# An adaLN, spectral-filter and bilinear-GLU block, forward and backward, on one core: TensorE's order in the tail written down as one chain, with filler dealt per step

## The chip, the cores and the metric

The kernel runs on one core of a Trainium2 chip. The metric is the time of one execution in microseconds of device time; where several executions were timed, the median is given. The engines are named as the profile names them: PE (TensorE, matmul), PEld (its weight loads), DVE (VectorE), ACT (ScalarE), POOL (GpSimd) and SP (SyncE, which here only issues transfers). "SPq" and "POOLq" are the queues of transfers that SP and POOL issue.

## The reference

The reference is the forward pass of one block and the gradients of all its inputs (jax.vjp), on x of 2048 rows by 576 columns in bfloat16, F = 4608:

```
mod = (silu(c) @ w_mod) split into sa, ca, ga, sb, cb, gb
h = layernorm(x) * (1 + ca) + sa
x = x + ga * irfft2(rfft2(h) * (w_r + i w_i))
h = layernorm(x) * (1 + cb) + sb
x = x + gb * (((h @ w_gate) * (h @ w_up)) @ w_down)
_out, _vjp = jax.vjp(_f, A_x, A_w_r, A_w_i, B_w_gate, B_w_up, B_w_down, c, w_mod)
```

The outputs are the result (out_0) and the gradients of x (out_1), w_r and w_i (out_2, out_3), w_gate and w_up (out_4, out_5), w_down (out_6), c (out_7) and w_mod (out_8).

## The kernel before, in words

The 2048 rows are 16 tiles of 128 (t = 0 to 15), the 4608 columns of the inner dimension 36 blocks of 128. All matmuls are bfloat16 with a 128 x 128 stationary tile. The Fourier transforms are matmuls with tables (T_RD, T_G, T_BD, T_BDA, T_GB, T_IR).

The first 284 us hold the norms, the forward transform and its filter, and the gradient that comes through w_down (u4p). From 284 to 1246.7 a loop runs over the 36 blocks: gate and up products (gup), the three weight-gradient products of earlier blocks (u57p, line 599: of hh, gg and gu, 32 matmuls each, 16 row tiles by two halves of 288 columns), and the gradient of the normed input (u8p, line 681), which VectorE adds into an f32 accumulator, line 686. Each block's hh goes out to DRAM (hhT_d), since the forward down projection needs all blocks.

What the change touches lies behind the last gate and up product:

- **The last accumulation**: the u8p of the last two blocks, together, for 16 tiles and 2 halves (128 matmuls, 32 additions on VectorE).
- **The backward norm**, a pipeline over the 16 tiles with four steps: `t1_norm` (loads of n2c, goc and yc on SP; norm gradient on VectorE and ScalarE), `t1_turn` (transposes trp, line 897; column sums csA, csB, csC, lines 800 and 807), `t1_cols` (products with T_RD, zp, line 917) and `t1_rows` (products with T_G, vp, lines 924 and 925). At t = 1 `t1_norm` also loads T_RD and multiplies its five slices by ga, line 885, on VectorE.
- **The held products**: the 192 u57p matmuls of the last two blocks are issued as filler beside the backward norm. Their outputs are cast by ScalarE and stored, those of gg and gu over a transposing transfer (woT, lines 610 to 612).
- **The spectral filter**, a pipeline over 19 chunks of four groups: `t2_turn` (transposes trv), `t2_filter` (xp; on VectorE products fm with the filter wn, line 198, which is loaded again from DRAM), `t2_back` (transposes), `t2_inv` (apt), `t2_grad` (for every fourth chunk the gradient of the filter, lines 963 to 972). The other 14 chunks' gradients are computed later (`more_grads`), beside the down projection.
- **The inverse transform**, a pipeline over 16 tiles with `t3_rows` (upa, upb), `t3_cols` (yp) and `t3_norm` (norm gradient, out_1, column sums csD, csE).
- **The down projection**: for each tile 72 matmuls (u3p, line 1129), two halves by 36 blocks. w_down lies in wdA (blocks 0 to 14) and wdB (15 to 35); hh comes back in pieces hl, four to two tiles, of nine blocks each. Then out_0, products for the gradient of gb, and `section`, which writes the six parts of the gradient of w_mod, five of them beside the projection (`late`) and the last at the very end.

The order on each engine comes from a planner of the tile framework: it takes instructions by priority (`tc.high_priority` with HEAD_START = 350 and SPREAD = 40 per step in the backward norm) and fills the gaps of one stage with ready work of another. `tc.issue_after(x)` keeps an instruction behind x. In the backward norm the list `fill` holds the last matmul of each group of held products, and `behind(fill[t - 1:t])` ties the zp of tile t to one of them, so that 16 held matmuls go between neighbours. SP's queue is in order: an issue that waits holds all behind it. The loads of hl and w_down are issued by SP, behind `after` (the yc load of tile 5):

```
wd_load(dst, k, f0, n, behind_=None):
    with tc.issue_after(behind_ or after):
        nc.sync.dma_start(dst[:, k:k + n, :], B_w_down[...])
```

Of the kernel before, what the change touches and what calls it, by code (L numbers as in the profile page):

```python
# [19 lines left out]
NT = 16  # L20
# [64 lines left out]
def build(ctx, tc, A_x, A_w_r, A_w_i, B_w_gate, B_w_up, B_w_down, c_in, w_mod, grad_out,  # L85
# [46 lines left out]


    cnt = [0]

# [51 lines left out]

    def pipeline(n, steps):

        for k in range(n + len(steps) - 1):  # L190
            for s_ in reversed(range(len(steps))):
                if 0 <= k - s_ < n:
                    steps[s_](k - s_)

    def spectral_products(m1, Z, wn, f0, w):
# [347 lines left out]
    with ExitStack() as ms:  # L543
# [14 lines left out]
        with ExitStack() as bs:  # L558
# [27 lines left out]
            nso = [0]  # L586
            fill = []

            def u57_items(sf, rhs_n, done):
                so = so4[:, nso[0] % NSO, :]  # L590
                nso[0] += 1
                items = []
                for h in range(2):
                    pw = []

                    def item(h, t, pw=pw):
                        if t == 0:
                            pw.append(u57ps.tile([128, 512], FP32, name="u57p", tag="x"))
                        mm = nc.tensor.matmul(pw[0][:, 0:288], lhsT=sf[:, t, :], rhs=rhs_n[:, t, h * 288:(h + 1) * 288], start=(t == 0), stop=(t == NT - 1))  # L599
                        if t == NT - 1:  # L600
                            fill.append(mm.ins)
# [124 lines left out]
            fill.clear()  # L726
# [9 lines left out]
    with ExitStack() as ts:  # L736
# [12 lines left out]
        zero = tl0.tile([128, 512], BF, name="zero")  # L749
        o2p = pool("o2p", 2)  # L750
        oAp = pool("oAp", 1)
        oBp = pool("oBp", 1)
# [38 lines left out]
        def wide(m):  # L791
# [64 lines left out]
        with ExitStack() as r1:  # L856
# [11 lines left out]
            def t1_norm(t):  # L868
                for k, src in (("n2c", n2_d), ("goc", go_v), ("yc", y_d)):
                    ld[k, t] = c1.tile([128, D], BF, name=k, bufs=5)  # L870
                    with behind(ld["order"]):
                        ins = nc.sync.dma_start(ld[k, t][:], src[:, t, :])
                if t == 5:
                    ld["after"] = ins.ins
                ld["final"] = ld["y", t] = ins.ins
                if t in (1, 2):
                    ld["order"] = [ins.ins]
                    with behind(ld["order"]):
                        for k, tag in ((("RD", "tA"),), (("G1", "tB"), ("BD2", None), ("BDA", None)))[t - 1]:
                            T[k] = load_table(tl0, k, tag)  # L880
                    ld["order"] = [tab_ins[k]]
                    if t == 1:
                        for m in range(5):
                            row = T["RD"][:, m].rearrange("p c f -> p (c f)")
                            nc.vector.tensor_scalar(out=row, in0=row, scalar1=ga_col[:, m:m + 1], scalar2=None, op0=MUL)
                n2 = ld["n2c", t][:]
# [24 lines left out]
            def t1_cols(t):  # L911
                zt = zts[t] = c1.tile([128, 2, FP], BF, name="zt")
                for cc in range(2):
                    zp = ps_fp.tile([128, 512], FP32, name="zp", tag="fp")
                    for m in range(5):
                        with behind(fill[t - 1:t] if t else []):
                            nc.tensor.matmul(zp[:, :FP], lhsT=gyTs[t][:, m, :], rhs=T["RD"][:, m, cc, :], start=(m == 0), stop=(m == 4))  # L917
                    nc.scalar.copy(zt[:, cc, :], zp[:, :FP])
# [10 lines left out]
            for k in range(NT + len(steps) - 1):  # L929
                with tc.high_priority(HEAD_START + SPREAD * k):  # L930
                    for s_ in reversed(range(len(steps))):
                        if 0 <= k - s_ < NT:
                            steps[s_](k - s_)
            after = ld["after"]
            dcb = diag_rows(tl, csA, csB, 288, "dcb")
# [10 lines left out]
        ra = pool("ra", 1, "right", stack=rA)  # L946
        wn = ra.tile([128, 2, NT, FP], BF, name="wn2")
        for c in range(2):
            with tc.issue_after(ld["final"]):
                nc.sync.dma_start(wn[:, c].rearrange("k a f -> k (a f)"), wn_d[:, c * NT * FP:(c + 1) * NT * FP])  # L950
        fg = pool("fg", 2, "right", stack=rA)
# [22 lines left out]
        with ExitStack() as r2:  # L974
# [95 lines left out]

        pipeline(NT, [t3_rows, t3_cols, t3_norm])
        dca = diag_rows(tl, csD, csE, 288, "dca")
# [8 lines left out]
        def more_grads(t):  # L1081
            for ci in rest[2 * (t - 2):2 * (t - 1)] if t >= 2 else []:
                with tc.issue_after(ld3["last"]):
                    filter_grad(ci)
            if t == 8:
                for which in range(2):
# [7 lines left out]

        late = {9: (MSB, of_sums(dsb)), 10: (MCB, of_rows(dcb)), 11: (MGA, of_rows(dga)), 12: (MSA, of_sums(dsa)), 13: (MCA, of_rows(dca))}


        csF = ps_cs.tile([128, 512], FP32, name="csF", tag="csB")
        wdA = oAp.tile([128, 15, D], BF, name="wdA")
        wdB = oBp.tile([128, NFB - 15, D], BF, name="wdB")  # L1100

        def wd_load(dst, k, f0, n, behind_=None):
            with tc.issue_after(behind_ or after):
                nc.sync.dma_start(dst[:, k:k + n, :], B_w_down[f0 * 128:(f0 + n) * 128, :].rearrange("(j f) d -> f j d", f=128))

        for k in range(0, 15, 5):
            wd_load(wdA, k, k, 5, ld["y", 7 + 2 * (k // 5)])
        prs = {}
        for tp_ in range(NT // 2):
            hls = []  # L1110
            for b0 in range(0, NFB, 9):
                nq = 4 * tp_ + b0 // 9
                hl = hlp.tile([128, 9, 256], BF, name="hl2") if nq >= 12 and (nq - 12) % 13 < 7 else o2p.tile([128, 9, 256], BF, name="hl", bufs=6)
                with tc.issue_after(after):
                    nc.sync.dma_start(hl[:], hhT_d[tp_, :, b0:b0 + 9, :])
                hls.append(hl)
                if tp_ == 0 and b0 in (9, 18):
                    wd_load(wdB, 10 * (b0 // 9 - 1), 15 + 10 * (b0 // 9 - 1), 9 + b0 // 9)
            x1t = o2p.tile([128, 2, D], BF, name="x1t3", bufs=1)
# [3 lines left out]
            for ti in range(2):  # L1123
                t = 2 * tp_ + ti
                ob = o2p.tile([128, D], BF, name="ob3")
                for h in range(2):
# [15 lines left out]
                more_grads(t)  # L1142
                if 8 <= t < 13:
                    for k in range(3 * (t - 8) if t < 12 else 12, min(16, 3 * (t - 7)) if t < 12 else 16):
# [84 lines left out]
```

## Time and profile before

| | |
|---|---|
| median of 3 runs | 1581.78 us (1580.73 to 1594.68) |
| the profiled execution | 1590.85 us |
| its span | 1589.1 us |
| PE busy | 1526.9 us (96%) |
| DVE busy | 1035.6 us (65%) |
| ACT busy | 551.5 us (35%) |
| POOL busy | 172.3 us (11%) |
| mean DMA rate over the span | 176 GB/s |
| mean granted PE clock | 0.993 |

The stages of the span begin at these times: last accumulation with the first norm steps 1246.7, the rest of the backward norm 1281.8, filter 1350.9, inverse transform 1413.9, down projection alone 1455.4, end section 1575.8.

In a row of the timeline the columns are start (us), duration (us), engine, line, operation, output and inputs, shape and count; in square brackets stands the idle time of the engine ahead of it and what ended it. Rows of groups have the summed busy time and the mean in ns, then the idle time ahead of the group's instructions. A busy PE is modelled: small gaps between matmuls do not show as idle. Windows give each engine's busy time, then the granted clock of PE as a share of full speed, the DMA engines' busy share and the rate.

### The profile page before, as it was taken

How to read it: one execution, taken by the hardware profiler on the slowest of the kernel's cores; microseconds unless marked ns; L12 is line 12 of the kernel's file. 1: busy time of each engine (PE TensorE's matmuls, PEld its weight loads, DVE VectorE, ACT ScalarE, POOL GpSimd, SP SyncE). 2: the span in 40 equal slices, each digit the busy share in tenths (PEclk: the TensorE clock that was granted, in tenths of full speed). 3: DMA queues.
4: the chain of work that ended last, by engine and by line, in shares of the span. 5: the costliest groups of instructions: out<-in, count | busy, mean ns of one | idle time of the engine just before them, and what ended most of it. 6: DMA issues, size and time to landing. Idle time of an engine off the chain costs nothing.

```text
span 1589.1 us, 30036 instructions
## 1 busy us (share of the span) xinstructions
PE 1526.9 (96%) x11299; PEld 1027.1 (65%) x11306; DVE 1035.6 (65%) x2632; ACT 551.5 (35%) x1136; POOL 172.3 (11%) x284
## 2 busy tenths in 40 slices
PE   6999889999999999999999999999999899899997
PEld 4666533566666676666667666666766566577775
DVE  6866653666666666666666666666666584678655
ACT  6667632322222222222222222222222255476022
POOL 0001212101010010101001010100100011100232
PEclk9999999999999999999999999999999999999998
DMA  9869998778778685785867777675856777646684
GB/s 319 270 196 245 238 242 227 159 150 148 143 140 164 125 168 116 162 155 113 166 136 150 146 151 135 145 160 115 169 122 131 204 200 211 234 151 224 244 239 143
DMA packets 491635, 280.19 MB, mean 176 GB/s; under 512 B 408897, under 2 KB 463810, under 8 KB 490466
## 3 DMA queue, kind: packets, MB, share of 16 engines
q1 hardware_dynamic: 466450, 187.75, 55.0%
q0 software_dynamic: 25040, 90.53, 19.0%
q8 instruction: 88, 1.44, 0.4%
q14 instruction: 57, 0.47, 0.1%
HBM read 108.33 MB, written 82.31 MB: 120 GB/s over the span
## 4 chain that ended last, share of the span: by engine, by line
PE 79%; DMA 9%; DVE 5%; issue 5%; ACT 1%; SPq 1%; POOL 0%; DVEq 0%; ACTq 0%; POOLq 0%
PE u57p L599 26%; PE u8p L681 18%; PE gup L652 16%; PE u4p L408 7%; PE u3p L1129 4%; PE gup L647 2%; DMA wdT<-wdn 2%; DMA Xn<-xn_d 2%; DMA wdB<-in_B_w_down_dram 1%; DMA xc<-in_A_x_dram 1%; DMA n2c<-n_d 1%; PE zp L346 1%; PE zp L917 1%; PE u4p L403 1%; DMA hh_sf<-hhT 1%
## 5 line engine op out<-in xcount | busy, mean ns | idle before, releaser
L686 DVE TENSOR_TENSOR acc<-acc,u8p 128x288 f32<-128x288 f32 x1088 | 489.3, 453 | 319.5 <-PE u8p L681 319.1
L681 PE MATMUL u8p<-wT,ggT 128*128 128x288 bf16 x1152 | 328.7, 287 | 4.4 <-DVE acc L686 4.4
L681 PE MATMUL u8p<-wT,guT 128*128 128x288 bf16 x1152 | 328.4, 287 | 0.0
L652 PE MATMUL gup<-h2T,wgu 128*128 128x512 bf16 x1152 | 294.9, 379 | 0.0
L602 ACT CAST so<-u57p 128x288 bf16<-128x288 f32 x216 | 86.0, 398 | 520.3 <-PE u57p L599 512.0
L599 PE MATMUL u57p<-h2p,gg_sf 128*128 128x288 bf16 x1152 | 189.2, 287 | 0.0
L599 PE MATMUL u57p<-gon,hh_sf 128*128 128x288 bf16 x1152 | 187.9, 286 | 0.3 <-DMA hh_sf<-hhT 0.3
L599 PE MATMUL u57p<-h2p,gu_sf 128*128 128x288 bf16 x1152 | 186.7, 286 | 0.0
L652 PEld LDWEIGHTS <-wgu 128*128 128x128 bf16 x1152 | 109.5, 98 | 98.8 <-issue 17.1
L408 PE MATMUL u4p<-goT,wdT 128*128 128x512 bf16 x656 | 152.7, 382 | 5.8 <-DVE ghh_st L143 5.3
L681 PEld LDWEIGHTS <-ggT 128*128 128x128 bf16 x1152 | 112.9, 98 | 67.4 <-issue 14.0
L681 PEld LDWEIGHTS <-guT 128*128 128x128 bf16 x1152 | 113.0, 98 | 58.4 <-issue 4.8
L1129 PEld LDWEIGHTS <-hl 128*128 128x128 bf16 x1152 | 112.0, 98 | 39.7 <-issue 10.4
L599 PEld LDWEIGHTS <-hh_sf 128*128 128x128 bf16 x1152 | 112.5, 98 | 28.9 <-DMA hh_sf<-hhT 0.6
L599 PEld LDWEIGHTS <-gg_sf 128*128 128x128 bf16 x1152 | 112.6, 98 | 28.5
L599 PEld LDWEIGHTS <-gu_sf 128*128 128x128 bf16 x1152 | 112.5, 98 | 28.5
L654 ACT CAST gT<-gup 128x512 bf16<-128x512 f32 x144 | 84.4, 586 | 130.7 <-PE gup L652 130.7
L408 PEld LDWEIGHTS <-wdT 128*128 128x128 bf16 x656 | 61.5, 98 | 79.1 <-issue 14.7
L654 ACT CAST uT<-gup 128x512 bf16<-128x512 f32 x144 | 84.3, 585 | 73.5 <-PE gup L652 73.5
L1129 PE MATMUL u3p<-wdB,hl 128*128 128x288 bf16 x672 | 92.7, 288 | 7.4 <-DMA wdB<-in_B_w_down_dram 7.4
L665 POOL DMA_DIRECT2D hhT_d<-hhT x36 | 33.2, 921 | 481.8 <-DVE hhT L656 452.8
L141 ACT CAST ghh_st<-u4p 128x512 bf16<-128x512 f32 x88 | 50.9, 585 | 65.3 <-PE u4p L408 64.3
(357 smaller groups left out, 1677.3 us busy)
## 6 DMA issues: line engine op xcount, KB each, us to landing
ghhT_d<-ghh_st POOLq DMA_DIRECT2D x36, 512.0 KB, 4.5
ghh<-ghhT_d POOLq DMA_DIRECT2D x36, 512.0 KB, 7.2
hhT_d<-hhT POOLq DMA_DIRECT2D x36, 512.0 KB, 6.5
hl<-hhT_d SPq DMA_DIRECT2D x32, 576.0 KB, 8.1
out_dram<-woT SPq DMA_DIRECT2D x72, 128.0 KB, 2.0
wdn<-in_B_w_down_dram SPq DMA_DIRECT2D x18, 288.0 KB, 3.6
out_dram<-so SPq DMA_DIRECT2D x36, 144.0 KB, 2.7
wgu<-in_B_w_gate_dram SPq DMA_DIRECT2D x18, 256.0 KB, 3.2
```

Source lines behind the costliest of these rows:

```text
L141: nc.scalar.copy(dst, src)
L346: mm = nc.tensor.matmul(zp[:, :FP], lhsT=hTs[t][:, m, :], rhs=T["RD"][:, m, cc, :], start=(m == 0), stop=(m == 4))
L408: nc.tensor.matmul(pt[:], lhsT=wdTs[k][:, j, m, :], rhs=goT[:, 4 * sb4:4 * sb4 + 4, m, :], start=(m == 0 and n == 5), stop=(m == n - 1))
L599: mm = nc.tensor.matmul(pw[0][:, 0:288], lhsT=sf[:, t, :], rhs=rhs_n[:, t, h * 288:(h + 1) * 288], start=(t == 0), stop=(t == NT - 1))
L602: nc.scalar.copy(so[:, h * 288:(h + 1) * 288], pw[0][:, 0:288])
L647: nc.tensor.matmul(pts[-1][:], lhsT=wgu[r, 8, jw * 128:(jw + 1) * 128], rhs=h2T[r, 4 * sb4:4 * sb4 + 4, 4, :], start=True, stop=False)
L652: nc.tensor.matmul(pts[k][:], lhsT=wgu[:, 4 * wi_ + m, jw * 128:(jw + 1) * 128], rhs=h2T[:, ts_, m, :], start=False, stop=(m == 3))
L654: nc.scalar.copy((gT, uT)[wi_][:, ts_, :], pts[k][:])
L665: nc.gpsimd.dma_start(hhT_d[:, :, fb, :].rearrange("tp f x -> f tp x"), hhT[:].rearrange("f (tp ti) p -> f tp (ti p)", ti=2))
L681: nc.tensor.matmul(pu[:, 0:288], lhsT=l_, rhs=r_, start=(k == 0), stop=(k == len(mms) - 1))
L686: nc.vector.tensor_tensor(out=dst, in0=dst, in1=pu[:, 0:288], op=ADD)
L1129: mm = nc.tensor.matmul(p2[:, 0:288], lhsT=hls[fb // 9][:, fb % 9, ti * 128:(ti + 1) * 128], rhs=(wdA[:, fb] if fb < 15 else wdB[:, fb - 1 ...
```

## The change

TensorE's order from the backward norm to the end of the inverse transform is written down. `pipeline` and the backward norm record, step by step, which PE instructions a step issues (`staged`); the held products (`held`) and the projections of tiles 0 to 5 (`proj`) are recorded too. `deal` then makes one sequence of them: to each step of the backward norm it adds 24, 16, 12 and from then on 10 filler matmuls, to each of the filter 12, and to the inverse transform 20 in the first step and 7 in each after it. `pe_order` ties each instruction to the one ahead of it. The ties through `fill` go.

- The held products are issued by kind (hh of both blocks, then gg, then gu) and no longer by block.
- wdB comes in three pieces of 7 blocks (10 and 11 before). These, wdA, the first four hl and the two halves of wn become one chain on SP in which each is kept behind the one ahead (`queued`, `last`): wdA in three, wdB 1, hl 0 to 3, wn in two, wdB 2 and 3, then the further hl.
- hl has buffers in two new pools (`hlg` 4, `hlh` 2) in place of six in `o2p`.
- The five scalings of T_RD run on POOL.
- The filter's pipeline has an empty step between `t2_filter` and `t2_back`.
- `more_grads` begins at tile 5 (2 before), its halving of two columns stands at tile 11 (8), the stores of the filter's gradient go four a tile at tiles 11 to 14 (three a tile from 8, the rest at 12), the `late` sections at tiles 8 to 12 (9 to 13).

```diff
+    def pe_order(seq):
+        for a, b in zip(seq, seq[1:]):
+            tc.add_manual_dep(b, a.name, mybir.DependencyInfo(mybir.DependencyClass.NoSync, ...), reason="order of PE")
...
+                if 0 <= k - s_ < n and steps[s_]:
+                    mark = traced()
                     steps[s_](k - s_)
+                    if stage:
+                        staged.append((stage, k, pe_since(mark)))
...
-            for fb_ in (NFB - 2, NFB - 1):
-                for i in range(3):
+            for i in range(3):
+                for fb_ in (NFB - 2, NFB - 1):
                     for f in product(fb_, i):
                         f()
+            held = pe_since(mark)
...
+        def deal(held, proj):
+            more, seq = held + proj, []
+            for n, (stage, k, ins) in enumerate(staged):
+                seq += ins
+                steps = sum(x[:2] == (stage, k) for x in staged)
+                at = sum(x[:2] == (stage, k) for x in staged[:n + 1])
+                if stage == 1:
+                    q = 24 if k == 0 else 16 if k == 1 else 12 if k == 2 else 10
+                else:
+                    q = 12 if stage == 2 else 20 if k == 0 else 7
+                q = q * at // steps - q * (at - 1) // steps
+                seq, more = seq + more[:q], more[q:]
+            pe_order(seq)
...
-                            nc.vector.tensor_scalar(out=row, in0=row, scalar1=ga_col[:, m:m + 1], scalar2=None, op0=MUL)
+                            nc.gpsimd.tensor_scalar(out=row, in0=row, scalar1=ga_col[:, m:m + 1], scalar2=None, op0=MUL)
...
-                        with behind(fill[t - 1:t] if t else []):
-                            nc.tensor.matmul(zp[:, :FP], ...)
+                        nc.tensor.matmul(zp[:, :FP], ...)
...
+        def queued(behind_, dst, src):
+            with behind([i_ for i_ in (behind_, last[0]) if i_ is not None]):
+                last[0] = nc.sync.dma_start(dst, src).ins
...
+        for k in range(0, 15, 5):
+            wd_load(k, 5, ld["y", 7 + 2 * (k // 5)])
+        wd_load(15, 7, ld["y", 12])
+        first_hl = [hl_load(nq, ld["y", 13 + nq // 2]) for nq in range(4)]
         for c in range(2):
-            with tc.issue_after(ld["final"]):
-                nc.sync.dma_start(wn[:, c]..., wn_d[...])
+            queued(ld["final"], wn[:, c]..., wn_d[...])
+        wd_load(22, 7)
+        wd_load(29, 7)
...
-            pipeline(NCH, [t2_turn, t2_filter, t2_back, t2_inv, t2_grad])
+            pipeline(NCH, [t2_turn, t2_filter, None, t2_back, t2_inv, t2_grad], 2)
...
-        pipeline(NT, [t3_rows, t3_cols, t3_norm])
+        pipeline(NT, [t3_rows, t3_cols, t3_norm], 3)
...
-            for ci in rest[2 * (t - 2):2 * (t - 1)] if t >= 2 else []:
+            for ci in rest[2 * (t - 5):2 * (t - 4)] if t >= 5 else []:
...
+                proj[t] = pe_since(mark)
+        deal(held, [i_ for t in range(6) for i_ in proj[t]])
```

More of the change, by code (lines that the diff above doesn't have):

```diff
@@ L131, in build, with traced, pe_since @@
         nc.vector.memset(pick[:, q, 64 * q:64 * q + 64], 1.0)
+    def traced():
+        return len(nc.cur_bb.bb.instructions)
+    def pe_since(mark):
+        return [i for i in nc.cur_bb.bb.instructions[mark:] if i.engine == mybir.EngineType.PE]
+    def pe_order(seq):
+        for a, b in zip(seq, seq[1:]):
+            tc.add_manual_dep(b, a.name, mybir.DependencyInfo(mybir.DependencyClass.NoSync, mybir.DependencyReason.DATA), reason="order of PE")
     cnt = [0]
@@ L586, in build @@
             nso = [0]
-            fill = []
             def u57_items(sf, rhs_n, done):
@@ L915, in t1_cols @@
                     for m in range(5):
-                        with behind(fill[t - 1:t] if t else []):
-                            nc.tensor.matmul(zp[:, :FP], lhsT=gyTs[t][:, m, :], rhs=T["RD"][:, m, cc, :], start=(m == 0), stop=(m == 4))
+                        nc.tensor.matmul(zp[:, :FP], lhsT=gyTs[t][:, m, :], rhs=T["RD"][:, m, cc, :], start=(m == 0), stop=(m == 4))
                     nc.scalar.copy(zt[:, cc, :], zp[:, :FP])
@@ L932, in build @@
                         if 0 <= k - s_ < NT:
+                            mark = traced()
                             steps[s_](k - s_)
-            after = ld["after"]
+                            staged.append((1, k, pe_since(mark)))
             dcb = diag_rows(tl, csA, csB, 288, "dcb")
@@ L1093, in store_grads @@
                 nc.gpsimd.dma_start((o2_v, o3_v)[which][:, a0:a0 + 2, :], wn[:, which, a0:a0 + 2, 0:DF])
-        late = {9: (MSB, of_sums(dsb)), 10: (MCB, of_rows(dcb)), 11: (MGA, of_rows(dga)), 12: (MSA, of_sums(dsa)), 13: (MCA, of_rows(dca))}
+        late = {8: (MSB, of_sums(dsb)), 9: (MCB, of_rows(dcb)), 10: (MGA, of_rows(dga)), 11: (MSA, of_sums(dsa)), 12: (MCA, of_rows(dca))}
         csF = ps_cs.tile([128, 512], FP32, name="csF", tag="csB")
[L1099 to L1108, printed above, removed]
-        for tp_ in range(NT // 2):
[L1110 to L1118, printed above, removed]
+        prs, proj = {}, {}
+        for tp_ in range(NT // 2):
+            hls = [first_hl[q] if tp_ == 0 else hl_load(4 * tp_ + q) for q in range(4)]
             x1t = o2p.tile([128, 2, D], BF, name="x1t3", bufs=1)
```

35 lines of the change are left out of this document (25 added, 10 removed).

## The prediction

> **What bounds the kernel now.** The whole edit lies behind the last gate and up product, so I read that stretch, 1246.66 to 1589.1, and first by stage (busy time of each engine in windows cut where the trace starts a stage: last w8 accumulation with the first norm steps, rest of the backward norm, start of the filter, rest of it, inverse transform, down projection, end).
>
> ```profile
> core 0: us, PE busy (x) PEld busy (x) DVE busy (x) ACT busy (x) POOL busy (x), PEclk, DMA share, GB/s
> 1246.66:1281.80 35.14, 30.56 (x225) 22.47 (x224) 24.77 (x68) 8.60 (x19) 3.08 (x5) 0.90 0.83 226
> 1281.80:1350.90 69.10, 64.16 (x605) 47.58 (x608) 45.18 (x123) 37.76 (x90) 11.64 (x23) 1.00 0.79 222
> 1350.90:1376.00 25.10, 17.37 (x166) 13.06 (x165) 11.86 (x34) 9.47 (x19) 2.57 (x6) 0.93 0.77 293
> 1376.00:1413.90 37.90, 37.20 (x383) 26.92 (x384) 31.13 (x96) 22.88 (x50) 4.78 (x9) 1.00 0.37 120
> 1413.90:1455.40 41.50, 40.32 (x377) 32.04 (x378) 36.75 (x105) 36.12 (x98) 0.00 (x0) 1.00 0.59 171
> 1455.40:1575.80 120.40, 117.77 (x938) 93.18 (x938) 71.97 (x184) 23.77 (x47) 32.28 (x54) 1.00 0.75 242
> 1575.80:1589.10 13.30, 2.20 (x7) 0.97 (x7) 7.65 (x18) 3.18 (x5) 4.83 (x3) 0.65 0.18 61
> ```
>
> TensorE sets the time and its work does not change, so only its losses can. A busy PE hides small gaps, hence I count its work by spacing: in dense runs of the timeline a matmul starts 0.1225 us after one of 288 columns, 0.124 after 292, 0.056 after 128, 0.11 after 256, 0.22 after 512, 0.03 after 64, and the twelve float sums take 0.49 each. The loops give 1728 matmuls of 288 columns, 224 of 292, 596 of 128, 64 of 256, 13 of 512 and 48 of 64: 289.9 us. The stretch lasts 342.4, so 52.5 us are lost, 12.1 of them in the end section, which the edit leaves alone. Where the other 40.4 go, by the timeline of TensorE and VectorE and the waits:
>
> ```profile
> 1259.66 1.50 DVE L885 TENSOR_SCALAR T_RD<-T_RD,ga_col 128x584 bf16<-128x584 bf16 x5 [4.39 <-DMA T_RD<-tab_RD]
> ```
> ```profile
> 1355.35 0.41 PE L1129 MATMUL u3p<-wdB,hl 128*128 128x288 bf16 x2 [2.65 <-DMA wdB<-in_B_w_down_dram]
> ...
> 1367.54 0.65 PE L1129 MATMUL u3p<-wdB,hl 128*128 128x288 bf16 x4 [4.76 <-DMA wdB<-in_B_w_down_dram]
> ```
> ```profile
> 1338.80 0.33 SPq L1115 DMA_DIRECT2D hl<-hhT_d  x1
> 1339.23 1.23 SPq L610 DMA_TRANSPOSE woT<-so  x1
> 1340.51 0.58 SPq L1115 DMA_DIRECT2D hl<-hhT_d  x1
> 1345.66 0.39 SPq L611 DMA_DIRECT2D out_dram<-woT  x1
> 1346.10 0.51 SPq L612 DMA_DIRECT2D out_dram<-woT  x1
> 1346.66 0.57 SPq L1104 DMA_DIRECT2D wdB<-in_B_w_down_dram  x1
> ...
> 1348.86 0.65 SPq L1104 DMA_DIRECT2D wdB<-in_B_w_down_dram  x1
> 1349.69 10.49 SPq L1115 DMA_DIRECT2D hl<-hhT_d  x3
> ```
>
> First row: the table scaling sits in VectorE's queue, waits 4.39 us for its table, and the accumulations of w8 behind it keep PE idle from 1259.06 to 1263.48. Second: the down projection stops twice for w_down. Third, SyncE's queue: the first hl is issued when the last held product ends (T0 = 1338.5), w_down's last piece 10.4 us later behind a transposed store whose load took 6.4, and it lands 18.6 us after its issue, at 1367.5, because 9.6 MB move from 1339 to 1368 and the DMA gave at most 413 GB/s.
>
> So three places: 14.8 us are lost before T0 (91.8 elapsed, 77.0 of work in the written order up to there), 11.7 from T0 to 1367.5 (29.1 elapsed, 17.4 of work), 13.9 behind that: 1.9 at a granted clock of 0.59 from 1369 to 1372, 4.6 in the rest of the filter, 4.3 in the inverse transform, 3.1 in the down projection.
>
> **The change, part by part.**
>
> *Table scaling on POOL.* VectorE no longer waits 4.39 us nor works 1.50. PE's idle 4.42 goes, and 3.0 us at half speed behind it (spacing 0.24 until 1269.6). Next is VectorE itself: 32 accumulations and the first norms, at 0.37 each and 3.5 a norm, so I keep 3 of that stage's 8.7 us as lost. On POOL five operations on 128x584 are not in the trace. Nearest are a 128x576 scaling and a 128x16 one:
>
> ```profile
> L850 POOL TENSOR_SCALAR o<-dmb,sc_col 128x576 bf16<-128x576 f32 x2 | 4.3, 2148 | 1.5 <-DVE dmb L143 1.5
> L1088 POOL TENSOR_SCALAR wn<-wn 128x16 bf16<-128x16 bf16 x4 | 1.6, 441 | 0.1
> ```
>
> Between 2.2 and 10.7 us for the five; I take 10.7, the row of nearly the same size. From 1259.7 that ends at 1270.4. The first zp needs it, and the written order puts 22.3 us of work ahead of it: 1269 plus 2 to 3 lost, about 1271.5. It just fits; twice as long would cost 9. Only gx_d stores stand behind it on POOL, read 150 us later.
>
> *Order and filler in the backward norm.* The 192 held products went 16 a step late in the stage (a step is 4.65 us: zp to zp 1320.06, 1324.68, 1329.33) while early steps ran at VectorE's 3.5 with n2c loads late twice (3.56 and 4.54 on the chain). Ten a step are 1.23 us beside 2.77 of the step's own, so 4.0: PE is ahead of VectorE's 3.5 all through. Cover for the n2c loads is that SyncE has no wn and no hl among them any more. I take 2.5 lost, with 1 to 7 as ends. T0 has 82.6 us of work ahead of it: 1246.7 + 82.6 + 5.5 = 1334.8, of 1331 to 1340.
>
> *Loads behind T0.* Here the edit gives back. The chained SyncE queue begins, past wdA, with a w_down piece whose buffer the last product still covers, so that it and all behind it (four hl, two halves of wn, two more w_down pieces) start at T0. Before, wn was on its way at 1316. And the last transposed store is still between them; what is queued behind its wait (6.4 us) is hl number 1 onward. Behind T0 SyncE brings 3.1 MB of w_down, 2.4 of hl, 2.4 of wn: 7.8 MB, and POOL brings 1.6 MB of table GB and 0.6 of x1 and grad_out. At 390 GB/s (window 1354 to 1362: 393) 10 MB take 25.6, and 2 to issue: the last piece lands at T0 + 27.6. TensorE has only 5.9 us of work before the projection step that needs it (number 29, among the twelve dealt to the first filter step). Lost: 21.7. Ends: 16, where only SyncE's 7.8 MB count and at 413 GB/s, with a little more than 2 of latency; and 28, where SyncE's own stall at a full queue (10.49 us for three hl) comes on top of the store's 6.4. Before, 17.4 us of work lay there, since xp, trv and projections of the first chunks were allowed past the stop; the written order allows nothing past. Where PE stands 4.4 us or more its clock falls (granted 0.62 in 1266 to 1270 behind 4.42, 0.59 behind 4.76, none behind 2.65): one such stop, 2.5.
>
> *Filter.* Twelve projections a step make it 48.2 us of PE work; VectorE needs 47.5 (19 steps of products, four of them with gradients). Near a tie: 4 lost, of 2 to 8. The empty step hides the way from fm to try. VectorE waited 8.8 us for xp's cast before; that it takes on the extra step costs one more step at the stage's end, counted in the 4.
>
> *Inverse transform.* Seven projections a step bring PE to 3.07 against VectorE's 2.51 (1425.76, 1428.28, 1430.79). 1.0 lost instead of 4.3.
>
> *Behind it.* 432 of the 1152 projections are done then, before 288. The next needs hl 12, whose buffer the inverse transform's last sums and norm still hold, and it stands on SyncE behind the stores of out_1 of the last two tiles. Before, 144 projections lay over that wait; now nothing does. Median hl from issue to landing: 8.1. I take 7 lost and 1.5 of clock, ends 0 and 12. The down projection itself loses 3 again: its stalls for Xn (10.9, 6.9, 7.1 us on the chain, few of them reaching PE) move with more_grads from t = 2 to t = 5, and the 16 wn stores, at 0.72 of POOL each, still end ahead of the last tile's store.
>
> *Products by kind, w_down in three.* No time of their own: the same products, and 1.03 MB pieces instead of 1.5.
>
> **Sum.** 5.5 + 21.7 + 2.5 + 4 + 1 + 8.5 + 3 + 12.1 (end) = 58.3 lost, against 52.5: plus 5.8. The profiled execution took 1590.85 (span 1589.1, 1.75 around it), 0.6% over the median 1581.78 of the three runs; I put the difference on the median: 1587.6, say 1587.
>
> **A rule against the change.** In the trace two-input operations of VectorE (L841, 128x576) that run inside POOL's two 2.15 us scalings at the end take 1.17 us in two cases, 0.76 in the others. So POOL slows VectorE by 0.4 us at most an operation, perhaps 2 us in all here, inside the 3 above. The Trainium skill, "SBUF — State Buffer", section "SBUF: two separate sides", says more: a VectorE operation with two SBUF inputs and a GpSimd operation hold the shared port pair by turns, each for its whole instruction. By that rule VectorE would stand up to 10.7 us, which is the third rival; the trace does not bear it out in full, as five VectorE operations passed beside two on POOL.
>
> **Rivals.**
>
> 1. *The loads keep up and PE runs full* (faster). The order takes the losses ahead of T0 down to 4, the last w_down piece lands at T0 + 21 (loss 15), no stop at hl 12. 4 + 15 + 2 + 2 + 0.5 + 0 + 2 + 12.1 = 37.6: minus 15, 1567. For it: DVE and POOL have room, and 413 GB/s were seen. Against: what is issued behind T0 is more than before, with less work over it.
> 2. *The queue behind T0* (slower). One chain on SyncE: each load behind the one before, the transposed store's wait and the full queue in series, so the last piece comes at T0 + 34 instead of 27.6. It decides from T0 + 31 or so. Loss 28, clock 4, filter 5, hl 12 with clock 12: 5.5 + 28 + 4 + 5 + 1 + 12 + 3 + 12.1 = 70.6, plus 18: 1600. For it: three hl issues that took 10.49 us. Against: pieces are smaller.
> 3. *POOL holds VectorE* (slower): 10.7 us where VectorE leads, minus 2 counted, so plus 8.7: 1596.
> 4. *The order does nothing*, since the old planner had nearly the same: about 1582. Against it is the count of projections, 432 against 288.
>
> **How the numbers follow.** A measurement tells 1% here, 15.8 us. Chances: forecast 0.53, rival 1 0.16, rival 2 0.18, rival 3 0.06, rival 4 0.07. Over 1% faster (below 1566): about half of rival 1 and some of the low ends, 0.14. Over 1% slower (above 1597.6): most of rival 2, a third of rival 3 and some high ends, 0.22. Within: 0.64. Range 1567 to 1603: rival 1's centre to a little past rival 2's. The forecast's own, 1577 to 1596.
>
> **What would show it.** T0 near 1335; no idle for T_RD on VectorE; zp(0) not waiting for POOL; norm steps of 4.0; the last w_down piece about 27 us behind T0 with PE idle some 20 before it; wn landing behind T0; a PE wait on hl at the end of the inverse transform. The prediction is wrong if PE's idle behind T0 is under 12 or over 30 us, if PE passes the inverse transform without that wait, or if steps of the filter run at VectorE's pace with PE idle in each.

## The result and the profile after

Over twelve executions of each, the changed kernel took 1601.74 us in the median (1594.14 to 1613.60), the kernel before 1584.17 (1579.22 to 1594.68). The ratio is 1.0107, with a 95% interval of 1.0080 to 1.0134: about 17 us slower. The profiled execution of the changed kernel took 1602.26 us, its span is 1600.5.

The span grew by 11.4 us only, because the stretch ahead of the edit ended 3.4 us earlier in this execution (1243.28 against 1246.66), in work that the edit does not touch. Later executions showed starts between 1238 and 1251, so from here on each trace is read from the last gate and up product. Counted so, the part that the edit touches lasted 342.4 us before and 357.2 after, plus 14.8.

Busy time by stage of the changed kernel (columns as before: window, length, then each engine's busy time and instructions, granted clock of PE, DMA share, rate). The windows are: norm steps, the wait behind the last held product (T0), the wait for w_down, the first filter steps, the rest of the filter, inverse transform, down projection.

```profile
core 0: us, PE busy (x) PEld busy (x) DVE busy (x) ACT busy (x) POOL busy (x), PEclk, DMA share, GB/s
...
1281.80:1334.00 52.20, 51.51 (x515) 41.32 (x513) 34.60 (x93) 33.19 (x76) 7.02 (x13) 1.00 0.64 161
1334.00:1344.60 10.60, 0.61 (x6) 0.24 (x5) 1.80 (x5) 0.70 (x2) 1.99 (x5) 0.76 0.90 234
1344.60:1369.00 24.40, 9.74 (x49) 5.94 (x50) 1.13 (x4) 1.79 (x4) 2.06 (x5) 0.64 1.00 374
1369.00:1378.00 9.00, 9.00 (x75) 7.08 (x73) 5.72 (x17) 4.04 (x8) 1.88 (x4) 0.74 0.30 103
1378.00:1421.50 43.50, 43.45 (x494) 37.34 (x493) 36.71 (x115) 30.73 (x63) 5.44 (x10) 1.00 0.39 125
1421.50:1474.80 53.30, 53.20 (x504) 44.13 (x505) 40.24 (x114) 37.63 (x99) 1.62 (x4) 1.00 0.49 151
1474.80:1587.30 112.50, 100.31 (x766) 77.67 (x766) 69.06 (x174) 21.63 (x42) 29.74 (x50) 0.95 0.75 243
```

The stages that the order was written for are full: PE is busy in all but 0.7 us of the norm steps, in 43.45 of 43.50 us of the filter's body and in 53.20 of 53.30 us of the inverse transform. Behind the first norm steps, and apart from the end section, most of the time is lost in two places. From 1334 to 1369, 35 us, PE is busy for 10.4, much of that at half clock; and the last stage has 12.2 us without work. The stops, in PE's timeline:

```profile
1344.59 1.38 PE L1168 MATMUL u3p<-wdA,hl 128*128 128x288 bf16 x5 [9.99 <-DMA hl<-hhT_d]
...
1365.76 1.84 PE L1168 MATMUL u3p<-wdB,hl 128*128 128x288 bf16 x7 [12.96 <-DMA wdB<-in_B_w_down_dram]
1368.62 0.88 PE L1168 MATMUL u3p<-wdB,hl 128*128 128x288 bf16 x3 [1.01 <-DMA wdB<-in_B_w_down_dram]
...
1482.35 3.78 PE L1168 MATMUL u3p<-wdA,hl 128*128 128x288 bf16 x15 [6.59 <-DMA hl<-hhT_d]
...
1527.74 3.42 PE L1168 MATMUL u3p<-wdA,hl 128*128 128x288 bf16 x15 [4.42 <-ACT ob L1169]
```

And SyncE's queue, which makes the first three:

```profile
1334.12 0.38 SPq L982 DMA_DIRECT2D wdB<-in_B_w_down_dram  x1
1334.61 1.21 SPq L623 DMA_TRANSPOSE woT<-so  x1
1335.87 0.71 SPq L982 DMA_DIRECT2D hl<-hhT_d  x1
1343.20 0.39 SPq L624 DMA_DIRECT2D out_dram<-woT  x1
1343.64 0.51 SPq L625 DMA_DIRECT2D out_dram<-woT  x1
1344.20 1.60 SPq L982 DMA_DIRECT2D hl<-hhT_d  x3
1345.86 1.11 SPq L982 DMA_DIRECT2D wn<-wn_d  x2
1347.01 5.41 SPq L982 DMA_DIRECT2D wdB<-in_B_w_down_dram  x2
```

T0 is 1333.9. The first w_down piece goes out 0.2 us behind it and the first hl 1.9 us behind it; that hl lands 8.7 us after its issue, and this ends the first stop. Then the queue stands 6.6 us, until the transposed transfer has landed and its store can go. SyncE issues nothing more in that time, and the rate from 1334.0 to 1344.6 is 234 GB/s. Three hl, both halves of wn and two w_down pieces follow, at 374 GB/s, and the last piece is there at 1368.6, T0 + 34.7. Before the change a hl went out at T0 + 0.3 and the last w_down piece landed at T0 + 29, with 17.4 us of PE work on the way; now there are 5.9.

The table scaling on POOL, the pace of the norm steps (POOL's gx_d stores mark them), and two VectorE operations beside the scaling:

```profile
1256.41 8.63 POOL L913 TENSOR_SCALAR T_RD<-T_RD,ga_col 128x584 bf16<-128x584 bf16 x5 [10.46 <-DMA T_RD<-tab_RD]
...
1290.42 0.54 POOL L920 DMA_DIRECT2D gx_d<-gxr  x1 [3.68 <-DVE gxr L805]
1294.64 0.54 POOL L920 DMA_DIRECT2D gx_d<-gxr  x1 [3.68 <-DVE gxr L805]
```
```profile
1258.22 0.83 DVE L804 TENSOR_SCALAR w<-n2c,ab 128x576 bf16<-128x576 bf16 x1
...
1260.08 1.15 DVE L800 SCALAR_TENSOR_TENSOR w<-gn,rstd2g,n2c 128x576 bf16<-128x576 bf16 x1
```

POOL takes 1.73 us for each of the five and ends at 1265.0; the first zp starts at 1271.2 and does not wait for it. VectorE's accumulations of w8 end 24.5 us behind the last gate and up product, 34.1 before. Most norm steps take 4.22 us.

### The profile page after: what moved, and what is told of

The parts are those of the page before. It is cut to its first block, busy times and chain, and to the rows that moved or that the text cites. A ratio compares the mean times of both kernels' runs of the same rounds, so it can differ in the third digit from the quotient of the medians.

```text
span 1600.5 us, 30060 instructions
## 1 busy us (share of the span) xinstructions
PE 1520.9 (95%) x11300; PEld 1031.5 (64%) x11306; DVE 1036.0 (65%) x2627; ACT 554.6 (35%) x1136; POOL 180.6 (11%) x289
## 4 chain that ended last, share of the span: by engine, by line
PE 79%; DMA 6%; issue 6%; DVE 5%; ACT 2%; POOL 1%; SPq 1%; POOLq 0%; ACTq 0%; DVEq 0%
PE u57p L613 26%; PE u8p L694 17%; PE gup L665 15%; PE u4p L424 6%; PE u3p L1168 6%; PE gup L660 2%; DMA Xn<-xn_d 2%; DMA wdB<-in_B_w_down_dram 1%; PE zp L944 1%; PE zp L362 1%; ACT u L798 1%; DMA ghhT_d<-ghh_st 1%; DMA hh_sf<-hhT 1%; DVE goT L395 1%; PE u4p L419 1%
## 5 line engine op out<-in xcount | busy, mean ns | idle before, releaser
L694 PEld LDWEIGHTS <-guT 128*128 128x128 bf16 x1152 | 112.7, 98 | 58.2 <-issue 5.0
L1168 PE MATMUL u3p<-wdB,hl 128*128 128x288 bf16 x672 | 101.3, 290 | 15.6 <-DMA wdB<-in_B_w_down_dram 14.0
L1168 PE MATMUL u3p<-wdA,hl 128*128 128x288 bf16 x480 | 77.8, 301 | 21.1 <-DMA hl<-hhT_d 16.6
```

Source lines behind the costliest of these rows:

```text
L694: nc.tensor.matmul(pu[:, 0:288], lhsT=l_, rhs=r_, start=(k == 0), stop=(k == len(mms) - 1))
L1168: mm = nc.tensor.matmul(p2[:, 0:288], lhsT=hls[fb // 9][:, fb % 9, ti * 128:(ti + 1) * 128], rhs=(wdA[:, fb] if fb < 15 else wdB[:, fb - 1 ...
```

## The experiments

Ratios are to the kernel before, run on the same chip; the changed kernel's is 1.0107 (1.0080 to 1.0134). "Tail" is the time from the last gate and up product's start to the end of the span in the one profiled execution: 342.6 before, 357.4 changed. The intervals reach 0.2% to 0.35% to each side, so two ratios less than some 0.4% apart are hardly told apart by the time alone; there the trace is read beside it, and each trace is one execution.

### wn out of the chain

```diff
+        for c in range(2):
+            with tc.issue_after(ld["y", 10]):
+                nc.sync.dma_start(wn[:, c]..., wn_d[...])
         wd_load(15, 7, ld["y", 12])
...
-        for c in range(2):
-            queued(ld["final"], wn[:, c]..., wn_d[...])
```

> The changed kernel with the two loads of wn taken out of the SP chain and issued beside the backward norm, ahead of the first w_down pieces. Theory (the SP chain behind the last held product is a matter of bytes): wn is 2.39 MB of what lies ahead of the last w_down piece; at the 374 GB/s seen there that is 6.4 us, so the last piece lands near T0 + 28.5 instead of T0 + 34.7, and the kernel gets 6 us faster than the changed one (ratio to before near 1.007). Rival (waits in series set it, the transposed store's 7.3 us and the latency of each load): PE's stop for w_down shrinks by under 2 us and the ratio stays at 1.0095 to 1.012; wn beside n2c, goc and yc may even delay T0 by 1 to 3 us.

Measured: 1.0068 (1.0042 to 1.0094), tail 349.5. PE's timeline of this kernel, whose T0 is 1332.2:

```profile
1352.79 1.06 PE L1169 MATMUL u3p<-wdB,hl 128*128 128x288 bf16 x7 [3.32 <-DMA wdB<-in_B_w_down_dram]
1359.29 0.88 PE L1169 MATMUL u3p<-wdB,hl 128*128 128x288 bf16 x3 [5.44 <-DMA wdB<-in_B_w_down_dram]
```

The last piece is there at T0 + 27.1 instead of 34.7, and the two stops for w_down fall from 13.97 to 8.76 us. T0 does not move (91.1 us behind the last gate and up product, 90.7 in the changed kernel), so wn costs nothing where it was taken to. The theory's 6 us are there, though the interval just overlaps that of the changed kernel; wn's place in the chain is part of the price.

### The last transposed store behind the loads

```diff
+        tc.add_manual_dep(turned_[-1], last[0].name, ...NoSync..., reason="order of SP")
```

Here `turned_` holds the transposing transfers of the held products, and `last[0]` is the third w_down piece.

> The changed kernel with the last held product's transposed store put behind the last w_down piece on SP, so that hl 1 to 3, wn and w_down no longer stand behind its wait. Theory (part of the 34.7 us from T0 to the last piece is SP waiting 7.3 us for that transfer, at 234 GB/s): the last piece lands 6 to 7 us earlier, near T0 + 28, ratio near 1.0065. Rival (bytes alone): the queue was never empty for long, the piece lands within 2 us of where it did, ratio 1.0095 or more.

Measured: 1.0062 (1.0038 to 1.0085), tail 351.9. SyncE's queue and PE's stop in this kernel, with T0 at 1331.4:

```profile
1331.55 0.38 SPq L984 DMA_DIRECT2D wdB<-in_B_w_down_dram  x1
1331.97 2.41 SPq L984 DMA_DIRECT2D hl<-hhT_d  x4
1334.43 0.92 SPq L984 DMA_DIRECT2D wn<-wn_d  x2
1335.40 7.82 SPq L984 DMA_DIRECT2D wdB<-in_B_w_down_dram  x2
1343.31 12.83 SPq L625 DMA_TRANSPOSE woT<-so  x1
```
```profile
1360.65 0.88 PE L1171 MATMUL u3p<-wdB,hl 128*128 128x288 bf16 x3 [0.85 <-DMA wdB<-in_B_w_down_dram]
```

All loads are issued by T0 + 12, and the last piece is there at T0 + 29.3, 5.4 us earlier. So bytes alone, as my sum had it, are not the price: the store's wait in the queue costs 5 us of it. The ratio is the one that the theory gave, its interval again just overlaps that of the changed kernel.

### All loads freed from T0

```diff
-        wd_load(15, 7, ld["y", 12])
         first_hl = [hl_load(nq, ld["y", 13 + nq // 2]) for nq in range(4)]
+        wd_load(15, 7, ld["y", 12])
...
-        wdB = oBp.tile([128, NFB - 15, D], BF, name="wdB")
+        wdB = [oBp.tile([128, 7, D], BF, name="wdB%d" % k) for k in range(3)]
```

besides wn as in the first experiment and the last two transposing transfers as in the second.

> The changed kernel with its loads no longer behind the last product: hl 0 to 3 ahead of wdB in the chain, wdB as three tiles so that each piece waits only for the buffers it lies on, wn beside the backward norm, the last two transposed stores behind the last piece. TensorE's written order is untouched. Theory (the wait behind T0 is the whole price of the change): only 1.03 MB are left for T0, the last piece lands near T0 + 6, PE's stops of 10.0, 13.0 and 1.0 us and the half clock behind them go, 25 to 30 us faster than the changed kernel, ratio 0.990 to 0.993. Rival: the DMAs cannot bring 7 MB more beside the backward norm, its loads of n2c, goc and yc come late and T0 moves by as much; ratio 1.000 or more.

Measured: 0.9979 (0.9947 to 1.0011), tail 348.6. In the trace the wait behind T0 is almost gone. PE starts its first projection 0.5 us behind T0 (10.7 before this edit), and the last piece is there at T0 + 9.4 after a stop of 3.27 us. T0 itself is where it was, 90.8 us behind the last gate and up product, so the DMAs do bring the other loads beside the norm steps. Since wdB is now three tiles, its first two pieces wait only for the products whose buffers they lie on; as one tile, the first waited for the very last product. That is the theory's mechanism, and the rival, a later T0, is out; but the gain is 20 us and not 25 to 30. In the profiled execution a new stop shows, in PE's and in VectorE's timeline:

```profile
1367.76 0.59 PE L829 MATMUL csF<-zero,ident 128*128 128x512 bf16 x1 [16.22 <-DVE dsb L968]
```
```profile
1360.62 0.69 DVE L844 TENSOR_TENSOR dcb<-csA,ident 128x512 f32<-128x512 f32 x1 [10.74 <-DMA woT<-so]
...
1367.25 0.46 DVE L968 COPY dsb<-csB 128x288 f32<-128x288 f32 x1 [5.08 <-DMA out_dram<-woT]
```

The tiles dcb and dsb lie on the buffers of the transposing transfers. VectorE, in order, waits until those have landed and been stored, csF waits for the bank that dsb frees, and PE's written order allows nothing past csF. This execution took 1593.94 us, 12.7 above the kernel's median, so the stop is probably not that long each time; no other execution was traced.

### The transposing transfers between the pieces

```diff
+        behind_sp(first_hl_ins, turned_[-2][0])
+        behind_sp(turned_[-2][0], wd_ins[15])
+        behind_sp(wd_ins[22], turned_[-1][0])
+        behind_sp(turned_[-1][0], wd_ins[29])
...
+            tl.tile([128, 400], FP32, name="gap")
             dsb = tl.tile([128, 288], FP32, name="dsb")
```

`behind_sp` fixes two instructions' order on SyncE; the stores go behind the third piece (for the last one, behind hl 5).

> The kernel with free loads again, with its last two transposing transfers put between the w_down pieces (the last one ahead of the third piece), their stores behind, and the tile dsb moved by 1600 bytes off the last transfer's buffer. In the free-loads kernel PE stood 16.2 us for dsb, since VectorE may write dsb only when the store of that buffer has landed. Theory (that stop was all that took the gain away): it goes, the end of the filter comes 14 to 16 us earlier, ratio 0.988 to 0.991. Rival (the transposing transfers take as long wherever they stand, and VectorE waits for the last one for dcb in any case): PE stops at csF for 5 us or more, ratio 0.995 or more.

Measured: 0.9947 (0.9926 to 0.9968), tail 329.9. The stop for dsb is down to 0.5 us in the trace, and the filter ends 148.0 us behind the last gate and up product, where it ended at 167.6 in the kernel above and at 176.3 in the changed one. So the stop went, as the theory had it, and the rival's wait at csF is not there. But the ratio is not the theory's (0.988 to 0.991), it lies at the edge of the rival's (0.995 or more), and the step of 0.3% from the kernel above is inside both intervals. The likely reason is that the forecast took the 16 us of one long execution for the usual: the shortest executions of the two kernels, 1570.8 and 1570.0 us, hardly differ, the longest, 1594.6 and 1583.5, do.

### Two stops in the last stage, alone

```diff
-            for ci in rest[2 * (t - 5):2 * (t - 4)] if t >= 5 else []:
+            for ci in rest[2 * (t - 2):2 * (t - 1)] if t >= 2 else []:
...
-        late = {8: (MSB, ...), 9: (MCB, ...), 10: (MGA, ...), 11: (MSA, ...), 12: (MCA, ...)}
+        late = {9: (MSB, ...), 10: (MCB, ...), 11: (MGA, ...), 12: (MSA, ...), 13: (MCA, ...)}
```

> The changed kernel with the rest of the filter gradients, the halving and the late sections back at the tiles where they were before (from tile 2, 8, and 9 to 13); the stores of the filter gradient stay at tiles 11 to 14. Theory: the PE stop of 4.42 us near 1523, with the half clock behind it some 5.5 us in all, comes from sections that now begin while VectorE still waits for Xn; it goes, ratio near 1.007. Rival: the chain of Xn loads reaches PE anyway at its own time, as 2.8 us of it did before; the stop moves and shrinks to about 3, ratio near 1.009.

Measured: 1.0087 (1.0063 to 1.0111), tail 351.5. The stop of 4.42 us for ob is gone from the trace, the largest wait on ob is 0.5, and nothing took its place (six other runs with the written order and the changed tiles have it too, at 3.4 to 4.9 us); from the inverse transform's last product to the last projection it is 107.2 us against 112.7. The time gained less than that (0.2%, within the interval), so the trace bears out the theory and the timing does not tell it from the rival.

```diff
-                    q = 12 if stage == 2 else 20 if k == 0 else 7
+                    q = 12 if stage == 2 else 20 if k == 0 else 5
...
-            pe_order(seq)
+            pe_order(seq + more)
```

> The changed kernel with five projections per step of the inverse transform in place of seven, the rest of the six tiles' projections behind the last step. Theory: 31 projections, 3.8 us, are then left to cover the wait for the hl piece that is loaded only behind the inverse transform; the stop of 6.6 us shrinks to about 3 and the half clock behind it goes, a step takes 2.8 us against VectorE's 2.5, so nothing is lost in the stage; 5 us faster than the changed kernel, ratio near 1.0075. Rival: the hl piece comes at a fixed distance behind VectorE's last store, and VectorE, not PE, sets that: the stage's end does not move, ratio as now (1.0107).

Measured: 1.0069 (1.0044 to 1.0094), tail 350.4. PE's timeline at the end of the inverse transform:

```profile
1481.95 4.25 PE L1168 MATMUL u3p<-wdA,hl 128*128 128x288 bf16 x20 [1.54 <-DMA hl<-hhT_d]
```

The 6.59 us are 1.54, with no loss in the stage itself, and the ratio is near the theory's (1.0075): what was dealt to the inverse transform beyond its need was the only cover for the load behind it.

### The table scaling, both ways

The changed kernel with the scaling back on VectorE:

```diff
-                            nc.gpsimd.tensor_scalar(out=row, in0=row, scalar1=ga_col[:, m:m + 1], scalar2=None, op0=MUL)
+                            nc.vector.tensor_scalar(out=row, in0=row, scalar1=ga_col[:, m:m + 1], scalar2=None, op0=MUL)
```

> The changed kernel with the table scaling back on VectorE. Theory (my step on the table): VectorE waits for T_RD again with the accumulations of w8 behind it, PE stands some 4.4 us and runs 3 us at half speed, T0 comes 4 to 6 us later and the kernel is 5 us slower than the changed one, ratio near 1.014. Rival: in the changed order VectorE reaches the table when it has nearly landed, or the work behind T0 is bound by loads that do not start at T0: ratio 1.0107 as now, within 0.002.

Measured: 1.0150 (1.0122 to 1.0178), tail 361.1. PE stops for VectorE as it did before the change:

```profile
1267.94 0.40 PE L694 MATMUL u8p<-wT,ggT 128*128 128x288 bf16 x1 [5.66 <-DVE acc L699]
```

T0 is 3.9 us later. So in the written order the move to POOL is worth about 4 us in the trace and 0.4% in time. The reverse edit in the kernel before, POOL alone:

> The kernel before with one part of the change alone: the five scalings of T_RD on POOL. Theory (one mechanism, whatever the order around it): VectorE's 4.39 us of waiting goes, PE's 4.42 us and the half speed behind it go, POOL needs 8.6 us as in the changed kernel; 5 to 6 us faster than before, ratio 0.9965. Rival: in the planner's order zp of tile 0 stood only 3 us behind the scaling; with 8.6 us on POOL PE now waits for POOL in place of VectorE, and the ratio is within 0.001 of 1.

Measured: 1.0022 (0.9994 to 1.0049), tail 342.6 as before. The theory's 0.9965 is out. The rival's mechanism is the one that the trace shows; its ratio, within 0.001 of 1, is missed by 0.001, with 1 inside the interval. PE's waits:

```profile
PE zp L917 <- POOL T_RD L885: 6.7, 5, 1.4
```

The planner's order puts the first zp right behind the table's landing, so PE waits for each of the five slices on POOL, 6.7 us, in place of 4.4 for VectorE. In these runs the move pays where the order puts the first zp some 15 us behind the table's landing (1256.4 to 1271.2 in the changed kernel).

### The written order, both ways

```diff
-            pe_order(seq)
+            del seq
...
-                        nc.tensor.matmul(zp[:, :FP], ...)
+                        with behind(fill[t - 1:t] if t else []):
+                            nc.tensor.matmul(zp[:, :FP], ...)
```

> The changed kernel without the written order: the old ties of the held products to zp are back, the planner orders TensorE; loads, pieces, products by kind, POOL and the later steps stay as changed. Theory (the written order keeps PE from other work while w_down is late, the loads are late by themselves): PE does part of the filter's transposes and products in the wait, as before, so from T0 to the last piece some 8 us less are lost, the stop at hl 12 goes too (7 us, 168 projections done behind the inverse transform); against that the backward norm loses 4 and the inverse transform 4 more: 5 to 8 us faster than changed, ratio 1.006. Rival (the written order is worth what it was written for): slower than the changed kernel, ratio 1.013 or more.

Measured: 1.0040 (1.0011 to 1.0069), tail 347.8. Without the written order the changed kernel is 0.7% faster. The loads are as late as before, the last piece lands at T0 + 36.1, but no stop for w_down shows: the planner puts 44 projections ahead of the first try, where the written order has 56, and lets transposes and products of the filter pass while the pieces are late. PE's longest stop is now for the filter's input, since wn stands in the same chain; the waits of PE and VectorE:

```profile
PE try__16720 L1065 <- DVE Ygc L1059: 8.5, 1, 8.5
```
```profile
DVE fm L214 <- DMA wn<-wn_d: 8.6, 2, 4.9
```

The filter ends 160.4 us behind the last gate and up product, 16 us earlier than in the changed kernel. Against that, T0 is 4.1 us later (PE waits 7.0 us for POOL's T_RD, as above). The same with the loads freed and the turns between:

> The kernel with free loads and the turns between, without the written order: the planner orders TensorE, with the old ties of the held products to zp. Theory (the written order is worth what it was written for only where the loads keep up; with late loads it cost 0.7%): without it this kernel gets slower by 4 to 8 us, ratio 0.997 to 1.000 against 0.9947. Rival (the free loads are the gain, the order adds nothing or still costs): ratio 0.9947 or lower.

Measured: 0.9962 (0.9937 to 0.9987) against 0.9947 (0.9926 to 0.9968) with the written order, tail 331.1 against 329.9. The difference, 0.15%, is inside both intervals and less than the theory's 0.997 to 1.000: with free loads the written order no longer costs, and whether it gains is not settled.

### All mends together

The free loads with the turns between, the old tiles for gradients and sections, five projections a step.

> The same kernel with the two mends measured alone before: filter gradients and sections back at their old tiles, and five projections a step in the inverse transform with the rest behind it. Theory (the stops are in different stages and add up; alone they gave 0.2% and 0.4%): 0.5 to 0.7% below the kernel without them, ratio 0.982 to 0.985. Rival (with the early stop gone the later ones move, since VectorE, SP and POOL come to them at other times): under 0.3% below, ratio 0.986 or more.

Measured: 0.9882 (0.9847 to 0.9917), 1566.8 us in the median of six against 1584.6: 1.2% faster than the kernel before and 2.2% faster than the changed one. The step from the kernel without the two mends is 0.65%, as the theory had it; the ratio forecast for the whole was too low because that of the kernel under it was. In the one trace the tail is 327.1, only 2.8 us less than in the kernel without the two mends: from the end of the inverse transform to the last projection 11 us less are lost, but the stop for the third piece is 7.8 us there against 2.3. So that the two gains add up rests on the medians and on that last stage. PE's remaining stops:

```profile
1345.30 0.88 PE L1187 MATMUL u3p<-wdB,hl 128*128 128x288 bf16 x3 [7.80 <-DMA wdB<-in_B_w_down_dram]
...
1455.25 2.62 PE L1187 MATMUL u3p<-wdA,hl 128*128 128x288 bf16 x20 [1.33 <-DMA hl<-hhT_d]
```

Products by kind were not undone by themselves. As I read the kernel, the first two pieces can come early because hh and gg are done first; that was not separated, nor were the three tiles of wdB from the order of the loads.

## Why the prediction was right and wrong

The time lies in the range, but only just: 1601.74 where 1587 was said and up to 1603 allowed, and beyond the forecast's own 1577 to 1596. It is what rival 2 gave (1600, with the last piece at T0 + 34; it came at T0 + 34.7), at a chance of 0.18. The signs that it named came: zp did not wait for T_RD, PE stood 24.7 us behind T0 (12 to 30 were the bounds), and it waited for hl at the end of the inverse transform. So the direction of the likeliest case was right and its size was not: I had the right place and part of the mechanism, at too small a price. Of rival 2's two causes the store's wait is shown; that a full queue held the last piece is not, since it was issued by T0 + 18.5 and landed 16 us later at 374 GB/s. That rival 2's sum comes so near is in part luck: it lost 9 us in the filter where 2.7 were lost, and 3 in the down projection where a wait unknown to it cost more. Losses in the profiled execution, counted from the last gate and up product in the way of the prediction:

| Place | predicted | measured |
|---|---|---|
| up to T0 | 5.5 | 8.1 (90.7 elapsed, 82.6 of work) |
| T0 to the last w_down piece | 21.7 | 28.8 (34.7 elapsed, 5.9 of work) |
| filter, with the half clock at its start | 6.5 | 2.7 |
| inverse transform | 1.0 | 0 |
| stop for hl 12 | 7 | 6.6 |
| half clock behind it, down projection | 4.5 | 9.2 |
| end section | 12.1 | 12.0 |
| sum | 58.3 | 67.4 |

The prediction's counts and spacings give 290.1 us of work, not 289.9; that moves the loss of both kernels by 0.2 us and decides nothing.

- *Loads behind T0* is the step that failed in size. It divided 10 MB by 390 GB/s as if the DMAs were full from T0 on. For the first 10.6 us they moved 2.48 MB, because SyncE stood behind the transposed store. I had named that wait (6.4 us) and put it only at the far end of the range. The bytes were short too: 11.6 MB moved from 1333 to 1369, since two more hl were issued before the last piece had landed. Taking the store out of the way brought 5.4 us, wn 7.6. The base of the step held: issued at T0, four hl, wn and w_down, with 5.9 us of work over them. With the loads freed the last piece landed 8.5 to 14 us behind T0 instead of 34.7.
- *Table on POOL* was right, T_RD 8.6 us (10.7 said) and done 6 us ahead of zp. Undone, it cost 4 us in the trace, for 5.7 forecast (8.7 lost before, 3 kept). That the gain hangs on the order, I had only half: I gave the time that zp leaves, not that the old order leaves none.
- *Up to T0*: the 2.6 us missing here are lost ahead of the first zp. It starts 27.9 us behind the last gate and up product with 22.3 of work ahead of it, so 5.6 were lost where I kept 3; PE's waits for VectorE there add up to 3.8. From the first zp to T0 2.5 were lost, as said, though the steps take 4.22 for 4.0: in eleven of the sixteen the ten zp take 1.46 or 1.47 us, in the others the 1.24 of a dense run, and the traces do not show why.
- *Filter*: 4 said, nothing measured beyond 2.7 us of half clock. At twelve projections a step PE, not VectorE, sets the pace, without loss.
- *Hl 12* was right to 0.4 us, and five projections a step, which the prediction did not have, were the remedy. (The kernel before had done 265 projections at the end of the inverse transform, not 288.)
- *Down projection* was wrong by a wait I did not see: I moved gradients and sections each by itself and asked only for room on POOL. Moved towards each other they overlap. Followed back from the stop, ob stands on ScalarE behind 2.2 us of a section, that behind a copy on VectorE, that behind products which wait for their load of grad_out (4.0 us), and this load starts only when VectorE has come through the gradients, where it had waited 2.5 us for Xn. PE waits 4.42 us for ob and then loses 1.4 at half clock.
- *The rule on the shared port*: beside the POOL scaling VectorE's operations took 0.83 instead of 0.42 and 1.15 instead of 0.81, some 1.5 us in all. That is near the 2 us said, and far from the 10.7 of rival 3. By the Trainium skill, "SBUF — State Buffer", section "SBUF: two separate sides", whichever starts first, a VectorE operation with two SBUF inputs or a GpSimd operation, holds the shared ports for its whole instruction. The trace bears out that the two engines hinder each other, and not that VectorE stands for the whole of each POOL instruction: its operation of 1.15 us, with two inputs, passed beside scalings of 1.73 us each.
- *Putting the profile's difference on the median*: the profiled execution of before was 6.7 us above the median of twelve, that of after 0.5 above. So plus 11.4 in the span is plus 17.6 in the medians. 3.4 of the 6.2 between them is the stretch ahead of the edit; the rest of the before execution's excess I can't place.

## What to carry to other kernels

A chain of loads written in the order of use is late as a whole when its first member waits, so order it by when each buffer comes free, give every piece its own tile, and put no store that waits for another transfer between loads. A written order for the bound engine removed small gaps here, and it also removed that engine's way past a late operand (0.7% with late loads, nothing that the time tells with loads on time): measure it with the loads on time. When filler is dealt out to the last one, ask what covers the next stage's first load.

## What was not expected of the hardware

- A transposing transfer of 160 KB that took 6.4 us before took 8.5 us here, issued between two plain loads. In the kernel with free loads two of them, issued behind seven loads, landed 15.4 and 22.2 us behind their issue.
- With the last transposed store behind the loads, SyncE issued 6.8 MB in 4.3 us, and then the issues themselves took long: 5.3 us for the last w_down piece, and 12.8 for a transposing transfer that waited for nothing else that the trace shows.
- The first 5.4 us of work behind a stop of 9.99 us ran at a granted clock of 0.52, and 8 us behind one of 12.96 at 0.50 to 0.53. The first cost nothing, since PE then waited again; the second is all that the filter lost.
